# Gated MLP: weight tasks cut into parts, one part in each half block, and the later parts of next x loaded later

## The chip, the cores and the metric

The kernel runs on one core of a Trainium2 chip. The metric is the device time of one execution in microseconds (us). TensorE multiplies matrices and writes its results to PSUM; VectorE and ScalarE read PSUM; GpSimd does not. Each engine works through its own queue in order. All loads and stores of the stage looked at here are issued from SyncE's queue (SP).

## The reference

```python
# attention with exponential features, 8 batches, 8 heads, 576 tokens, 64 wide
num = einsum('bhsf,bhfd->bhsd', phi(q), einsum('bhsf,bhsd->bhfd', phi(k), v))
x = num / (einsum('bhsf,bhf->bhs', phi(q), phi(k).sum(2))[..., None] + 1e-06)   # -> (8, 576, 512)
# gated MLP
h = maximum(x @ w_in, 0)                       # 512 -> 1024
u, v = h[..., :512], h[..., 512:]
v_n = (v - mean(v)) / sqrt(var(v) + 1e-06)
v_s = einsum('ts,bsd->btd', w_spatial, v_n) + b_spatial[None, :, None]
x = (u * v_s) @ w_out                          # 512 -> 512
# mixer
u = x + (x.transpose(0, 2, 1) @ U @ V).transpose(0, 2, 1)     # rank 32 over the tokens
out = u + maximum(u @ w_ch1, 0) @ w_ch2                       # 512 -> 2048 -> 512
```

`w_in`, `w_out`, `U`, `V`, `w_ch1` and `w_ch2` come as 64-bit floats, the rest as 32-bit floats. The kernel turns the doubles into 32-bit floats on the chip. Products are taken in the rounded format `float32r`; each operand is split into a high and a low part, and three products (high high, high low, low high) are summed.

## The kernel before, in words

There are three stages: attention, the gated MLP (with the low-rank mixing), and the channel products with `w_ch1` and `w_ch2`. The change lies in the second, `gated_mlp`, which runs over the eight batches; its instructions are issued in the order in which the code writes them.

One batch of it has these steps on TensorE. `gate` computes **pu** (u = relu(x w_in)): four blocks f of 128 columns, each in two half blocks c of 288 tokens, 12 matmuls each. ScalarE evicts each half block (line 948). Then it computes **pz**, the spatial product: again four blocks in two halves, 14 matmuls each (lines 833 and 968). VectorE multiplies pz by u (line 972), ScalarE casts the product to its high part g, and GpSimd subtracts to get the low part; for the last block VectorE does that. Then comes **px**, the product with w_out in five token tiles, the low-rank sums **pr**, the values **pv** of the *next* batch between them (`ahead`), and `mixed`, which transposes (pt), adds the low-rank part (py) and stores u (tile `uo` to `ud`). The results pu, pz, px, pv and pt go to one pool of four PSUM banks: TensorE stops when the fourth result back has not been read.

In the second half of `gate` the next batch's x is loaded: four parts x32 of 128 rows, with two buffers; ScalarE casts each to its high part (line 872) and GpSimd subtracts the low part (line 869).

Beside this work the weights of the channel stage are prepared. `units` lists **tasks**, and seven of them are worked off in each batch: one behind each block of pu (`self.work()` in `gate`), one behind the first px tiles, and two in `mixed` (called m1 and m2 here). The kinds of task are:

- a *raw* task: 128 x 512 doubles, loaded to `raw` or `raw2` in turn by `fetch`, then turned into floats by `repack_doubles`: two ScalarE passes (`low`, line 110, and the size, line 112), then four VectorE passes (lines 113, 117, 120, 121). The tiles `low`, `bits` and the result `w32` have one buffer each. The result is stored to `w1d` or `w2r`, or kept in `w2`;
- `low_rank` and `v_stack`: the doubles of U and V, repacked, then copied to the stacked tiles ua, ub, vs;
- `pair(m)` and `left(m)`: sums of weight blocks on GpSimd (`left_sums`, tile z2) and their split into high and low parts (the tile of tag `w2s`, one buffer), stored to `w2d` and `w1x`. These are the operands of the fast block products of the channel stage.

A task's instructions all stand at one point. `flush` issues the stores that are due and then the loads of the next two raw tasks. It is called behind the first half block of each pu block and at two points behind pz, so SP's queue takes stores, raw loads and loads of x in that order.

After the last batch's pz, `first_chunk` loads u of the first chunk, `load_left` loads four weight tiles cw, and the channel stage's first products `hidden` (ph_x, ph_y, ph_z) start between the last batch's px and pt.

Of the kernel before, what the change touches and what calls it, by code (L numbers as in the profile page):

```python
# [9 lines left out]
F32 = mybir.dt.float32  # L10
# [90 lines left out]
def repack_doubles(nc, pool, dst, raw, name):  # L101


    n = dst.shape[1]
    pair = raw[:, : 2 * n].rearrange("p (c two) -> p c two", two=2)
    lo, hi = pair[:, :, 0], pair[:, :, 1]
    low, bits = (
        pool.tile([P, PIECE], I32, tag=t, name=f"{t}_{name}", bufs=1)[:, :n] for t in ("low", "bits")
    )
    nc.scalar.activation(low, lo.bitcast(U32), AF.Copy, scale=2.0**-29)  # L110
    size = lo.bitcast(F32)
    nc.scalar.activation(size, hi.bitcast(F32), AF.Square)
    nc.vector.tensor_scalar(
        out=bits, in0=hi, scalar1=3, scalar2=0x3FFFFFF8,
        op0=ALU.logical_shift_left, op1=ALU.bitwise_and,
    )
    nc.vector.scalar_tensor_tensor(
        out=bits, in0=hi, scalar=-0x40000000, in1=bits, op0=ALU.bitwise_and, op1=ALU.bitwise_or
    )
    nc.vector.tensor_tensor(out=bits, in0=bits, in1=low, op=ALU.add)  # L120
    nc.vector.scalar_tensor_tensor(
        out=dst, in0=size, scalar=TINY * TINY, in1=bits.bitcast(F32), op0=ALU.is_ge, op1=ALU.mult
    )


class Mixer:
# [175 lines left out]
    def fetch(self, parts, name):  # L302


        nc, raw = self.nc, None
        if any(src.dtype != F32 for _, src in parts):
            tag, pool = (("raw", self.sp), ("raw2", self.mq))[self.fetched % 2]
            self.fetched += 1
            raw = pool.tile([P, 2 * PIECE], I32, tag=tag, name=f"{tag}_{name}", bufs=1)
            for view, src in parts:  # L310
                nc.sync.dma_start(view(raw, 2), src.bitcast(I32))

        def into(dst):
            if raw is not None:
                return repack_doubles(nc, self.sp, dst, raw, name)
            for view, src in parts:
                nc.sync.dma_start(view(dst, 1), src)
        return into

    def units(self):  # L320


        nc, R, NF, HS, tail = self.nc, self.R, self.NF, self.HS, self.tail
        units = []

        def low_rank():
            c0, c1 = NF * R, (NF + 1) * R
# [1307 lines left out]
```

## Time and profile before

| | before |
|---|---|
| median of 3 runs | 1616.64 us (1614.0 to 1617.75) |
| the profiled execution | 1615.92 us |
| its span | 1614.1 us |
| TensorE busy | 1560.1 us, 97% of the span, 11592 matmuls |
| VectorE busy | 1112.1 us, 69% |
| ScalarE busy | 874.9 us, 54% |
| GpSimd busy | 797.2 us, 49% |
| DMA | 336.87 MB, mean 209 GB/s |

The span is the time between the first and the last instruction that the profiler saw, and the execution's own time is 1.8 us longer. "Busy" is the sum of instruction times of an engine. Ends of matmuls are modelled, so a busy TensorE need not be at its peak; a gap in its row is a real wait.

### The profile page before, as it was taken

What the parts mean: (1) busy time and instruction counts of PE and PEld (TensorE: products, weight loads), DVE (VectorE), ACT (ScalarE), POOL (GpSimd) and SP (SyncE); (2) the same over time, 40 slices, a digit from 0 to 9 for tenths busy, and PEclk for the clock granted to TensorE, in tenths of its full rate; (3) what the DMA queues carried; (4) which work ended last, traced back from release to release, by engine and by line L of the source; (5) the groups of instructions that cost most, each with busy time, mean ns of one, the idle gap of its engine ahead of it and who ended that gap; (6) DMA issues with size and microseconds to landing.
All of it is one profiled execution on the core that took longest, in us unless ns stands there. A gap on an engine that the chain in (4) does not pass through costs nothing.

```text
span 1614.1 us, 30569 instructions
## 1 busy us (share of the span) xinstructions
PE 1560.1 (97%) x11592; PEld 1469.5 (91%) x11592; DVE 1112.1 (69%) x1628; ACT 874.9 (54%) x1656; POOL 797.2 (49%) x610
## 2 busy tenths in 40 slices
PE   7999999998999999989999999999999999999998
PEld 7998888987888888878889999999999999999998
DVE  5888866875577677665675767777776666666656
ACT  4878768874444444434444555555554555554542
POOL 2677776775334343443523544455643533344433
PEclk9999999999999999999999999999999999999999
DMA  4677666753243343442526788989999877777786
GB/s 129 175 207 210 190 199 181 201 165 111 89 149 109 115 138 123 138 162 83 187 94 250 258 286 283 307 286 315 309 312 388 264 248 232 242 240 247 247 249 231
DMA packets 172278, 336.87 MB, mean 209 GB/s; under 512 B 25826, under 2 KB 96610, under 8 KB 169060
## 3 DMA queue, kind: packets, MB, share of 16 engines
q1 hardware_dynamic: 171988, 334.86, 65.0%
q8 instruction: 91, 1.49, 0.4%
q14 instruction: 55, 0.45, 0.1%
q10 hardware_dynamic: 144, 0.07, 0.0%
HBM read 251.73 MB, written 73.55 MB: 202 GB/s over the span
## 4 chain that ended last, share of the span: by engine, by line
PE 72%; DVE 9%; DMA 8%; ACT 4%; issue 3%; POOL 2%; SPq 1%; DVEq 0%; ACTq 0%; POOLq 0%
PE pc L833 19%; PE ph_x L833 11%; PE ph_z L833 6%; PE px L833 5%; PE pv L833 4%; PE pz L833 4%; PE pn L666 4%; PE pkv L638 3%; PE ph_y L833 3%; DMA den<-nd 2%; PE pu L833 2%; PE pk L565 2%; PE pt L597 1%; PE pq L565 1%; DMA raw_c<-in_w_ch 1%
## 5 line engine op out<-in xcount | busy, mean ns | idle before, releaser
L833 PE MATMUL pc<-hc,w 128*128 128x288 f32 x2688 | 423.2, 295 | 4.7 <-ACT hc L171 1.9
L833 PEld LDWEIGHTS pc<-hc,w 128*128 128x128 f32 x2688 | 379.0, 188 | 5.9 <-ACT us L171 2.1
L619 POOL TENSOR_TENSOR qp<-e,qp 128x576 fp32r<-128x576 f32 x128 | 183.5, 1455 | 118.7 <-ACT e L616 93.2
L833 PE MATMUL ph_x<-us,cw 128*128 128x288 f32 x1536 | 241.9, 295 | 0.1
L833 PEld LDWEIGHTS ph_x<-us,cw 128*128 128x128 f32 x1536 | 216.1, 188 | 1.0 <-ACT u L1272 0.5
L174 DVE TENSOR_TENSOR hc<-h,hc 128x576 fp32r<-128x576 f32 x192 | 191.8, 1002 | 34.1 <-ACT hc L171 34.0
L666 PE MATMUL pn<-qp,kv 128*65 128x288 f32 x768 | 207.1, 330 | 6.0 <-ACT nd L677 2.6
L1205 POOL TENSOR_TENSOR h<-h,h 128x576 f32<-128x576 f32 x64 | 108.0, 1690 | 132.2 <-DVE r L1441 126.2
L1205 POOL TENSOR_TENSOR t<-u,t 128x576 f32<-128x576 f32 x32 | 57.6, 1801 | 197.9 <-DVE c L1277 182.0
L638 PE MATMUL pkv<-v,kp 128*128 128x65 f32 x1024 | 154.6, 254 | 0.0
L638 PEld LDWEIGHTS pkv<-v,kp 128*128 128x128 f32 x1024 | 153.2, 193 | 0.0
L1272 ACT COPY u<-ph_x 128x288 f32<-128x288 f32 x128 | 51.1, 399 | 182.3 <-PE ph_x L833 182.3
L833 PE MATMUL ph_z<-us,cw 128*128 128x288 f32 x768 | 123.2, 296 | 10.0 <-DVE c L1277 10.0
L171 ACT CAST hc<-h 128x576 fp32r<-128x576 f32 x192 | 128.4, 672 | 6.6 <-PE pc L833 3.6
L1287 ACT ACTIVATE h<-c 128x288 f32<-128x288 f32 x192 | 85.2, 444 | 83.9 <-DVE c L1277 83.9
L833 PE MATMUL pz<-wt,vn 128*128 128x288 f32 x768 | 115.7, 300 | 11.6 <-DVE u L972 7.4
L833 PEld LDWEIGHTS pz<-wt,vn 128*128 128x128 f32 x768 | 107.7, 192 | 13.8 <-DVE u L972 8.4
L833 PEld LDWEIGHTS ph_z<-us,cw 128*128 128x128 f32 x768 | 108.4, 188 | 11.9 <-DVE c L1277 11.8
L904 POOL TENSOR_TENSOR rstd<-rstd,mhalf 128x1 f32<-128x1 f32 (+1 forms) x40 | 30.1, 753 | 168.6 <-DVE rstd L903 168.6
L666 PEld LDWEIGHTS pn<-qp,kv 128*65 128x65 f32 x768 | 99.2, 139 | 12.0 <-ACT nd L677 5.1
L833 PE MATMUL pu<-xs,wi 128*128 128x288 f32 x768 | 104.9, 298 | 4.9 <-ACT u L948 4.9
L833 PEld LDWEIGHTS pu<-xs,wi 128*128 128x128 f32 x768 | 104.3, 191 | 5.9 <-ACT u L948 5.1
(166 smaller groups left out, 3085.6 us busy)
## 6 DMA issues: line engine op xcount, KB each, us to landing
w<-w2d SPq DMA_DIRECT2D x224, 512.0 KB, 4.8
u<-ud SPq DMA_DIRECT2D x16, 1152.0 KB, 8.2
raw_c<-in_w_ch SPq DMA_DIRECT2D x32, 512.0 KB, 4.0
cw<-w1x SPq DMA_DIRECT2D x8, 1792.0 KB, 13.8
v<-in_v SPq DMA_DIRECT2D x32, 325.0 KB, 4.2
k<-in_kT SPq DMA_DIRECT2D x32, 320.0 KB, 3.5
q<-in_qT SPq DMA_DIRECT2D x32, 320.0 KB, 3.7
x<-nd SPq DMA_DIRECT2D x64, 144.0 KB, 3.3
```

The source lines that it names most:

```text
L171: self.put(nc.scalar.copy(hi, src))
L174: return self.put((nc.gpsimd if elo == "pool" else nc.vector).tensor_tensor(out=lo, in0=src, in1=hi, op=ALU.subtract))
L565: self.pin(nc.tensor.matmul(pa[:, j * NF + t, :], x[d, t * P : (t + 1) * P], ws[d, :], start=True, stop=True,))
L597: self.pin(nc.tensor.transpose(pt[:, at, :], s[:, u, :], self.ident))
L619: self.pin(nc.gpsimd.tensor_tensor(out=lo[:, c], in0=e[:, c], in1=hi[:, c], op=ALU.subtract))
L638: self.pin(nc.tensor.matmul(pkv[:, i, j, :], kp[:, j * NF + t, :], vb[:, u * D1 : (u + 1) * D1], start=False, stop=(j == 1 and t == NF - 1),))
L666: self.pin(nc.tensor.matmul(pn, kv[k][:, i, g // 2, :], qp[q][:, i, g * HS : (g + 1) * HS], start=(m == 0), stop=(m == len(terms) - 1),))
L833: self.put(self.nc.tensor.matmul(out, x, y, start=(start and i == 0), stop=(stop and i == len(terms) - 1), skip_group_check=chained,))
L904: nc.gpsimd.tensor_tensor(out=rstd[:n], in0=rstd[:n], in1=self.mhalf[:n, :1], op=ALU.pow)
L1205: x = self.put(self.nc.gpsimd.tensor_tensor(out=out, in0=p, in1=q, op=ALU.subtract))
L1272: self.put(nc.scalar.copy(out, src))
L1287: self.put(nc.scalar.activation(self.h[n, t // 2, x][:, t % 2], src, AF.Relu))
```

## The change

Each task is cut into parts, and each part gets a fixed place. A batch has the places 0 to 7 (the half blocks of pu), 8 to 15 (those of pz), "x" and "blocks" behind the first px tiles, and m1 and m2 in `mixed`. `work(b, place)` issues what the plan holds for that place.

- `repack_doubles` becomes the class `Repack` with `words` (the two ScalarE passes), `bits` (the first two VectorE passes) and `into` (the last two).
- `units` fills the plan: raw tasks mostly at the places (3, 4, 5), (6, 7, 8), (9, 10, 11), (12, 13, 14). Splits are cut into a high and a low part. U's copies stand at places 6 and 7 of batch 0, V's at 8 and 9. `left` and `pair` of a group are spread over three batches.
- `flush` is called behind every half block, and `work` after it.
- `normalize` is called behind the second half of each pu block, as before, and the small `pad` task moves from ahead of batch 0 to its place 3.
- The loads of parts 2 and 3 of next x stand behind the second half of pz blocks 1 and 2; they stood behind blocks 0 and 1.

```diff
-def repack_doubles(nc, pool, dst, raw, name):
...
+class Repack:
...
+    def words(self):
+        nc = self.nc
+        self.low, self.size = self.tile("low"), self.lo.bitcast(F32)
+        nc.scalar.activation(self.low, self.lo.bitcast(U32), AF.Copy, scale=2.0**-29)
+        nc.scalar.activation(self.size, self.hi.bitcast(F32), AF.Square)
+
+    def bits(self):
...
+        nc.vector.tensor_scalar(
+            out=bits, in0=hi, scalar1=3, scalar2=0x3FFFFFF8,
...
+        nc.vector.scalar_tensor_tensor(
+            out=bits, in0=hi, scalar=-0x40000000, in1=bits, op0=ALU.bitwise_and, op1=ALU.bitwise_or
+        )
+
+    def into(self, dst):
+        nc = self.nc
+        nc.vector.tensor_tensor(out=self.b, in0=self.b, in1=self.low, op=ALU.add)
+        nc.vector.scalar_tensor_tensor(
...
     def units(self):
...
+        def raw(load, b, places, store):
+            u = {}
+            def begin():
+                u["s"] = load()
+            self.raws.append([begin, False])
+            entry = self.raws[-1]
+            def end():
+                store(u["s"][2])
+                self.raws.remove(entry)
+            for place, f in zip(places, (lambda: u["s"][0](), lambda: u["s"][1](), end)):
+                at(b, place, f)
...
+        def halves(src):
+            d, n = self.mq.tile([P, 2, 4, HALF], F32R, tag="w2s", name=f"w2s_{self.made}", bufs=1), 0
...
+            def high():
+                for k, x in spans:
+                    nc.scalar.copy(d[:, 0, k], x)
+            def low():
+                for k, x in spans:
+                    nc.vector.tensor_tensor(out=d[:, 1, k], in0=x, in1=d[:, 0, k], op=ALU.subtract)
+            return d, n, high, low
...
         def pair(m, b, places):
...
+            at(b, 15, sums)
+            dst = lambda i, x: self.w2d[0][:, x, m, i, :]
+            part(lambda: [w[0][:, :, :HALF], w[0][:, 1, HALF:]], dst, 0, b, (15, "x"))
+            part(lambda: [z[0]], dst, 3, b, ("m1", "m1"))
...
         def left(m, b):
...
+            at(b, "blocks", load)
+            at(b, "m2", sums)
+            dst = lambda i, x: self.w1x[0][:, m, i, x]
+            part(lambda: [w[0][:, :3]], dst, 0, b, ("m2", "m2"))
+            part(lambda: [z[0]], dst, 3, b + 1, (2, 3))
...
+        usual = ((3, 4, 5), (6, 7, 8), (9, 10, 11), (12, 13, 14))
         half = self.DC // 2
+        raw(lambda: self.fetch(parts, "uv", c1 + HS), 0, (2, 4, 5), low_rank)
+        at(0, 3, self.pad)
+        at(0, 6, lambda: u_copies(0))
+        at(0, 7, lambda: u_copies(1))
+        at(0, 8, lambda: v_stack(0))
+        at(0, 9, lambda: v_stack(1))
+        first, others = columns(0) + columns(half), columns(PIECE) + columns(half + PIECE)
+        for x, places in zip(first, ((9, 10, 11), (12, 13, 14), ("m1",) * 3, ("m2",) * 3)):
+            piece(*x, 0, places)
+        for x, places in zip(first[4:], usual):
+            piece(*x, 1, places)
         for m in range(GROUP):
...
+            left(m, m + 1)
+            pair(m, m + 2, usual[:2])
+            for x, places in zip(others[2 * m : 2 * m + 2], usual[2:]):
+                piece(*x, m + 2, places)
+        for i in range(2):
+            for t in range(GROUP):
+                piece(*rows(GROUP + t + i * self.NM), 6 + i, usual[t])

     def flush(self):
...
+        for u in self.raws[:2]:
+            if not u[1]:
+                u[1] = True
+                u[0]()
+
+    def work(self, b, place):
+        for f in self.plan.pop((b, place), ()):
+            f()
...
                 nc.scalar.activation(u[:, c, :], pu[:, :HS], AF.Relu)
-                if c == 0:
-                    self.flush()
-            self.normalize()
+                self.flush()
+                if c:
+                    self.normalize()
+                self.work(b, 2 * f + c)
             us.append(u)
-            self.work()
...
-            if loads[f]:
-                loads[f]()()
-                if f + 2 < KD:
-                    loads.append(load(f + 2))
-            else:
-                loads.append(None)
+                self.flush()
+                if c and 1 <= f < KD - 1:
+                    loads.append(load(f + 1))
+                if c and loads[f]:
+                    loads[f]()()
+                self.work(b, 8 + 2 * f + c)
...
-            self.work()
+            self.work(b, "x")
             for t in range(NST):
...
                 if t == 1:
                     self.flush()
+                    self.work(b, "blocks")
...
             self.mixed(b, ts, t1, range(KD // 2))
-            self.work()
+            self.work(b, "m1")
```

Three places in the program show how the order moves. The first is ScalarE in pu of batch 1, before the change: line 948 evicts pu, lines 110 and 112 are the first passes of a raw task.

```order
L948 ACTIVATE u_0_5419<-pu_0_1_5437 128x288
L110 ACTIVATE low_c_1_1024_5456<-raw_c_1_1024_5346 128x512
L112 ACTIVATE raw_c_1_1024_5346<-raw_c_1_1024_5346 128x512
L948 ACTIVATE u_1_5464<-pu_1_0_5465 128x288
L948 ACTIVATE u_1_5464<-pu_1_1_5482 128x288
L110 ACTIVATE low_c_2_1024_5497<-raw_c_2_1024_5435 128x512
L112 ACTIVATE raw_c_2_1024_5435<-raw_c_2_1024_5435 128x512
L948 ACTIVATE u_2_5505<-pu_2_0_5506 128x288
```

The same stretch of ScalarE after the change (the lines are now 988, 116 and 117):

```order
L988 ACTIVATE u_0_5407<-pu_0_1_5425 128x288
L988 ACTIVATE u_1_5443<-pu_1_0_5444 128x288
L988 ACTIVATE u_1_5443<-pu_1_1_5458 128x288
L116 ACTIVATE low_c_0_1024_5472<-raw_c_0_1024_5334 128x512
L117 ACTIVATE raw_c_0_1024_5334<-raw_c_0_1024_5334 128x512
L988 ACTIVATE u_2_5475<-pu_2_0_5476 128x288
L988 ACTIVATE u_2_5475<-pu_2_1_5493 128x288
L988 ACTIVATE u_3_5510<-pu_3_0_5511 128x288
L116 ACTIVATE low_c_1_1024_5528<-raw_c_1_1024_5423 128x512
```

Two tasks instead of four begin in this pu, three evictions apart.

The second place is VectorE where pz of batch 1 begins. Before, four whole tasks stand ahead of the first product out of pz (line 972); these are the last rows of the fourth:

```order
L121 SCALAR_TENSOR_TENSOR w_c_3_1024_5537<-raw_c_3_1024_5480,bits_c_3_1024_5539 128x512
L113 TENSOR_SCALAR bits_c_0_0_5580<-raw_c_0_0_5521 128x512
L117 SCALAR_TENSOR_TENSOR bits_c_0_0_5580<-raw_c_0_0_5521,bits_c_0_0_5580 128x512
L120 ISA bits_c_0_0_5580<-bits_c_0_0_5580,low_c_0_0_5579 128x1024
L121 SCALAR_TENSOR_TENSOR w_0_5578<-raw_c_0_0_5521,bits_c_0_0_5580 128x512
L972 TENSOR_TENSOR u_0_5419<-pz_0_0_5593,u_0_5419 128x288
L972 TENSOR_TENSOR u_0_5419<-pz_0_1_5611,u_0_5419 128x288
L972 TENSOR_TENSOR u_1_5464<-pz_1_0_5633,u_1_5464 128x288
```

After, with line 1012 for the product and 122, 126, 132, 133 for the passes:

```order
L122 TENSOR_SCALAR bits_c_1_1024_5545<-raw_c_1_1024_5423 128x512
L126 SCALAR_TENSOR_TENSOR bits_c_1_1024_5545<-raw_c_1_1024_5423,bits_c_1_1024_5545 128x512
L1012 TENSOR_TENSOR u_0_5407<-pz_0_0_5554,u_0_5407 128x288
L132 ISA bits_c_1_1024_5545<-bits_c_1_1024_5545,low_c_1_1024_5528 128x1024
L133 SCALAR_TENSOR_TENSOR w_c_1_1024_5572<-raw_c_1_1024_5423,bits_c_1_1024_5545 128x512
L1012 TENSOR_TENSOR u_0_5407<-pz_0_1_5575,u_0_5407 128x288
L1012 TENSOR_TENSOR u_1_5443<-pz_1_0_5601,u_1_5443 128x288
L122 TENSOR_SCALAR bits_c_2_1024_5619<-raw_c_2_1024_5526 128x512
L126 SCALAR_TENSOR_TENSOR bits_c_2_1024_5619<-raw_c_2_1024_5526,bits_c_2_1024_5619 128x512
L1012 TENSOR_TENSOR u_1_5443<-pz_1_1_5622,u_1_5443 128x288
```

At most two passes stand between two products out of pz.

The third place is SP's queue around the end of batch 7: the last weight stores (to w2r), the load of the first chunk (u from ud) and the first cw. Before:

```order
L1051 DMA ud_71<-uo_3_2_9375 128x320
L481 DMA w1x_89<-w1s_1_9379 128x1024 x2
L481 DMA w2r<-w_c_15_9441 128x512
L1201 DMA u_0_9698<-ud_65 128x2304
L1142 DMA cw_9700<-w1x_89 128x3584
```

After:

```order
L1091 DMA ud_71<-uo_3_2_9346 128x320
L529 DMA w2r<-w_c_12_9471 128x512
L330 DMA raw_c_14_9490<-in_w_ch 128x1024
L529 DMA w2r<-w_c_13_9531 128x512
L330 DMA raw_c_15_9553<-in_w_ch 128x1024
L529 DMA w2r<-w_c_14_9597 128x512
L529 DMA w2r<-w_c_15_9661 128x512
L1241 DMA u_0_9698<-ud_65 128x2304
L1182 DMA cw_9700<-w1x_89 128x3584
```

Four stores of batch 7's own tasks, the last one issued behind place 14, now stand ahead of the load of u; before, one task was left for that batch.

## Rows read from the trace of the kernel before

**Rows 1.** TensorE's waits, 380 to 920 us: us in total, times, longest.

```profile
PE pz L833 <- DVE u L972: 7.4, 4, 5.1
PE pu L833 <- ACT u L948: 4.9, 1, 4.9
PE pz L833 <- ACT u L948: 4.2, 4, 1.5
...
PE px L833 <- POOL g L174: 1.9, 1, 1.9
```

**Rows 2.** Busy time by window: length, PE, PEld, DVE, ACT, POOL, clock, DMA.

```profile
386.48:452.92 66.44, 61.53 (x358) 54.82 (x357) 43.54 (x88) 30.69 (x69) 24.19 (x23) 0.97 0.26 84
452.92:517.42 64.50, 60.52 (x359) 53.35 (x357) 46.79 (x88) 27.53 (x57) 25.37 (x26) 1.00 0.36 122
517.42:578.20 60.78, 60.12 (x358) 53.24 (x357) 42.19 (x79) 26.95 (x55) 23.52 (x24) 1.00 0.37 118
578.20:639.52 61.32, 60.37 (x359) 53.37 (x358) 43.35 (x83) 27.21 (x56) 25.73 (x26) 1.00 0.43 136
639.52:700.73 61.21, 60.26 (x359) 53.32 (x357) 43.62 (x79) 26.54 (x55) 22.89 (x24) 1.00 0.41 128
700.73:768.89 68.16, 63.07 (x359) 56.13 (x357) 41.48 (x79) 26.51 (x54) 28.70 (x30) 0.95 0.42 144
768.89:832.45 63.56, 61.65 (x359) 54.26 (x357) 40.45 (x75) 26.68 (x54) 28.04 (x28) 0.97 0.40 131
832.45:860.02 27.57, 27.57 (x209) 27.57 (x208) 15.04 (x27) 8.06 (x18) 9.35 (x11) 1.00 0.30 113
485.25:517.42 32.17, 32.17 (x152) 25.70 (x150) 23.53 (x47) 14.40 (x30) 13.68 (x14) 1.00 0.25 85
```

**Rows 3.** The same view, the stretch behind batch 5's longest wait.

```profile
726.10:732.50 6.40, 6.36 (x27) 6.36 (x28) 1.54 (x4) 3.04 (x7) 5.87 (x7) 0.51 0.18 48
```

**Rows 4.** Timeline of ScalarE and VectorE, six moments: start, us, instruction [idle before, releaser].

```profile
399.36 0.32 ACT L352 CAST ua<-w_uv 128x160 fp32r<-128x160 f32 x1 [7.52 <-DVE w_uv L121]
...
462.52 1.51 DVE L113 TENSOR_SCALAR bits_c<-raw_c 128x512 int32<-128x512 int32 x1
...
465.62 0.67 ACT L110 ACTIVATE low_c<-raw_c 128x512 int32<-128x512 uint32 x1 [5.73 <-DVE bits_c L120]
...
699.06 0.84 ACT L171 CAST w1s<-w 128x768 fp32r<-128x768 f32 x1
...
723.90 0.83 ACT L171 CAST w1s<-w 128x768 fp32r<-128x768 f32 x1 [9.57 <-DMA raw_c<-in_w_ch]
...
794.53 0.68 ACT L872 CAST xs<-x 128x576 fp32r<-128x576 f32 x1 [4.82 <-DMA x<-xd]
```

**Rows 5.** Passes on raw tiles, 380 to 872 us: ns min/median/max.

```profile
L113 DVE TENSOR_SCALAR bits_c<-raw_c x32: 414/427/1508, 403.9 to 840.5; 128x512 int32<-128x512 int32 x32
L117 DVE SCALAR_TENSOR_TENSOR bits_c<-raw_c,bits_c x32: 691/693/1821, 404.4 to 842.1; 128x512 int32<-128x512 int32 x32
...
L121 DVE SCALAR_TENSOR_TENSOR w_c<-raw_c,bits_c x24: 691/693/1051, 406.2 to 843.7; 128x512 f32<-128x512 f32 x24
```

**Rows 6.** Groups by line and shape, VectorE, 380 to 870 us: busy us, mean ns.

```profile
L972 DVE TENSOR_TENSOR u<-pz,u 128x288 f32<-128x288 f32 x64 | 27.4, 452 | 45.1 <-PE pz L968 45.1
```

**Rows 7.** Timeline of GpSimd and VectorE behind pz of batch 1.

```profile
487.83 1.47 POOL L869 TENSOR_TENSOR xs<-x,xs 128x576 fp32r<-128x576 f32 x1 [0.49 <-ACT xs L872]
488.02 1.82 DVE L117 SCALAR_TENSOR_TENSOR bits_c<-raw_c,bits_c 128x512 int32<-128x512 int32 x1
```

**Rows 8.** DMA issues, 380 to 870 us: count, KB each, median us to landing.

```profile
w1x<-w1s SPq DMA_DIRECT2D x8, 512.0 KB, 5.2
```

**Rows 9.** End of batch 7: DMA issue of u (845 us), and timeline of SP, ScalarE.

```profile
u<-ud SPq DMA_DIRECT2D x1, 1152.0 KB, 5.1
...
860.26 1.82 SPq L1142 DMA_DIRECT2D cw<-w1x  x4
...
862.04 1.24 ACT L171 CAST us<-u 128x576 fp32r<-128x576 f32 x2
```

More of the change, by code (lines that the diff above doesn't have):

```diff
@@ new lines, in units, with at @@
+        self.raws, self.stores, self.waiting, self.plan = [], [], [], {}
+        def at(b, place, f):
+            self.plan.setdefault((b, place), []).append(f)
+        def raw(load, b, places, store):
[9 more added lines that the diff above has]
+                at(b, place, f)
@@ new lines, in units, with piece, store @@
+        whole = lambda t, s: t[:, : s * PIECE]
+        def piece(dst, src, name, b, places):
+            def store(into):
+                w = self.stage(name, PIECE)
+                into(w)
+                self.stores.append((dst, w))
+            raw(lambda: self.fetch([(whole, src)], name, PIECE), b, places, store)
+        parts = [(
+            lambda t, s: t[:, : s * c0].rearrange("p (k r) -> p k r", k=NF),
+            self.U[: NF * P, :].rearrange("(k p) r -> p k r", p=P),
+        )]
@@ new lines, in units, with part, first, second @@
+        self.made = 0
+        def part(src, dst, x0, b, places):
+            h = {}
+            def first():
+                h["d"], h["n"], high, h["low"] = halves(src())
+                high()
+            def second():
+                h["low"]()
+                for i in range(2):
+                    self.stores.append((dst(i, slice(x0, x0 + h["n"])), h["d"][:, i, : h["n"]].bitcast(F32)))
+            at(b, places[0], first)
+            at(b, places[1], second)
+        def pair(m, b, places):
@@ L386, in pair, with store @@
             w, z = [], []
-            def load(i):
+            for i in range(2):
                 r = slice((m + i * self.NM) * P, (m + i * self.NM + 1) * P)
-                into = self.fetch([(whole, self.w_ch2[r, :])], f"c2_{m}_{i}")
-                def step():
+                def store(into, i=i):
                     if i == 0:
@@ L446, in left, with sums @@
-            return [("blocks", load, True), (None, lambda: part(1), False)]
-        def rows(m):
-            return [
-                ("raw", piece(self.w2r[:, kk, :], self.w_ch2[kk * P : (kk + 1) * P, :], f"c2_{kk}"), False)
-                for kk in (m, m + self.NM)
-            ]
+            def sums():
+                z.append(self.mq.tile([P, 4, HALF], F32, tag="z2", name=f"z1_{m}", bufs=1))
+                self.left_sums([w[0][:, x] for x in range(4)], z[0])
+            at(b, "blocks", load)
@@ L1070, in gated_mlp @@
                 self.flush()
-                assert not self.todo
+                assert not self.plan and not self.raws
                 right.close()
```

233 lines of the change are left out of this document (81 added, 152 removed).

## The prediction

> **What bounds the kernel now.** I read the page first: TensorE is busy 97% of the span, so only time in which it waits or runs at a low clock can be won. The change lies in the gated MLP, about 386 to 875 us, so I next listed what TensorE waited for there, then cut that stretch into batches, then looked at the engines that were waited for.
>
> The waits of TensorE inside the stage that the change could touch are 7.4 + 4.9 + 4.2 + 1.9 = 18.4 us, all at evictions: pz waits until VectorE has multiplied an older pz out of its bank (line 972), pu and pz wait until ScalarE has evicted a pu (line 948), px for a low part on GpSimd [rows 1]. The windows run from the first pu matmul of one batch to that of the next [rows 2]. The last batch runs its pu and pz in 27.57 us with TensorE busy all the time, and the rest of a period takes 32.17 us in batch 1, again without a gap. A period without waits is thus 59.74 us. The seven periods are 66.44, 64.50, 60.78, 61.32, 61.21, 68.16 and 63.56 us, so they hold 6.70 + 4.76 + 1.04 + 1.58 + 1.47 + 8.42 + 3.82 = 27.8 us too much. That is more than the 18.4 us of waits, because the clock falls too: behind the longest wait, 5.1 us in batch 5, the granted clock is 0.51 for 6.40 us, the 1.2 GHz level instead of 2.4 [rows 3].
>
> Why an eviction is late is seen on the engine in front of it [rows 4]. ScalarE takes its queue in order. In batch 0 it stands 7.52 us before the copies of the low-rank weights, with finished pu blocks behind it. In batch 1 it stands 5.73 us before the first step of a weight task, which needs a buffer that VectorE still reads. In batch 5 it stands 9.57 us before a cast. The releaser named there is a raw load; by the code the cast writes the one buffer w2s, whose former content was still being stored, so I trust the place and not the name. In batch 6 it stands 4.82 us for a load of next x. In every case a whole weight task was put between two pu blocks, its first step waited, and evictions stood behind it.
>
> **The change part by part.** Call the 16 half blocks of a batch places 0 to 15: 0 to 7 are pu (12 matmuls each), 8 to 15 pz (14 each). 208 matmuls in 27.57 us make 0.1326 us each, so 1.59 us a place in pu and 1.86 in pz. T0 is the first pu of a batch.
>
> *No work is added.* The plan issues the same ScalarE, VectorE and GpSimd steps and the same DMAs; only their order differs. So the sum consists of waits that go and waits that come.
>
> *Waits that go.* A task's words (two ScalarE passes), bits (two VectorE passes) and the rest (two more) now stand one place apart. Nothing that waits in line for its data has a long chain in front: the buffer `low` is free again when the third part of the last task is done, one place before the next words. In batch 1 the fast times of the four VectorE passes are 0.43 + 0.69 + 0.69 + 0.69 us (for the third I take the time of the second) [rows 5], 2.50 us a task, and one product out of pz is 0.45 us [rows 6]. In batch 1 VectorE comes to its first pass behind the last token tile's normalisation at 462.52 us, T0 + 9.6 [rows 4]; with the two tasks before place 8 it comes to T0 + 14, where the first pz ends at T0 + 14.6. In pz it then has 8 x 0.45 for products, 7.5 - 1.1 for three tasks of which one has begun, and 2 x 0.45 (the same shape) for low parts of the last gated block, 10.9 of 14.84 us. It fits, so VectorE is late by no more than single places, and TensorE has four banks, that is three places or 5.6 us, before lateness reaches it. I count all 27.8 us as removed, and then what comes.
>
> *Batch 0.* u_copies still waits for the repacked low-rank weights, at 399.4 us as now, but it stands behind pu block 6 instead of blocks 2 to 7; only block 7 waits, about 1 us, within the banks. 0.5 us is left for the clock and small gaps.
>
> *Collisions in pz, batches 1 to 6.* A VectorE pass beside GpSimd's low parts can be much longer: a 0.69 us pass took 1.82 us when GpSimd began its x part 0.19 us before it [rows 7]. Three tasks a batch that lay mostly in pu now lie partly beside GpSimd's ten passes in pz. With some 0.4 us on each of ten passes VectorE needs 14.9 us instead of 10.9, as long as pz itself; what lateness comes of it the banks hide. I take 0.3 us a batch, 1.8 us; bounds 0 and the rival below.
>
> *The buffer w2s in batches 2 to 4.* It has one copy. In these batches the second half of a pair is split at m1, the first half of the next left weights at m2 and their second half at places 2 and 3, each waiting until the stores of the one before have landed. A pair of those stores takes 5.2 us at the larger size [rows 8]. In batch 5 ScalarE came to the cast that stood at m2 at 699.06 us, 1.7 us before T0 [rows 4]. VectorE's low part at m1 lies before that in the order, some 2 to 4 us before T0 (an estimate), so the stores land at T0 + 1.2 to 3.2, ScalarE stands 3 to 5 us and the evictions behind it come by T0 + 4. TensorE needs the bank of the last pv at T0 + 4.8. Hidden, narrowly; I take 0.4 us a batch, 1.2 us; bounds 0 and 4 a batch.
>
> *Next x.* Parts 2 and 3 are loaded two places before they are used, and no longer stand with part 0 and 1 in SP's queue. A load landed on time in the good batches, and a late one holds up only ScalarE's casts g and the low parts of the last block, which px needs only after its first 27 matmuls. The cost is 0; it takes away batch 6's wait, where the loads came late.
>
> *SP at the end of batch 7.* Now one weight task ends at place 14 of the last batch. Its store stands in SP's queue ahead of the load of the first chunk u and of the four cw loads. u used to be issued at T0 + 13, right after pu, and landed in 5.1 us; cw at 860.26 us, when pz ended [rows 9]. The last pz but one ends 1.86 us before pz does; a product, its cast and low part (0.45 each, by the product's row) and two passes of 0.69 follow, so VectorE ends that task about 1 us after pz, u goes out at pz + 1.4 and lands at pz + 6.5, and cw starts 1.6 us later behind 1152 KB of u. ScalarE's cast us<-u at 862.04 us, pz + 2, now waits until pz + 6.5 with the eviction of px behind it, GpSimd's sums begin as late, and I estimate that VectorE's chain of low parts up to the fifth hidden product ends 0.5 to 2 us later than TensorE wants it. The cw loads come some 4 us later; how much they have in hand no row shows, so 0 to 4. I take 1.3 us in all; bounds 0 and 6.
>
> Sum: -27.8 + 0.5 + 1.8 + 1.2 + 1.3 = -23.0 us. The profiled execution of 1615.92 us (span 1614.1 and 1.8 around it) becomes 1592.9. It lies 0.72 below the median of the runs, so against the median of 1616.64 the forecast is 1593.6 us.
>
> **The rivals.**
>
> *Forecast (0.76):* the waits go and small ones remain, 1588 to 1600 us.
>
> *The waits only move (0.15).* w2s lands late in batches 2 to 4 (two waits, 2 us each, 12 us) or the end of batch 7 costs its 6 us instead of 1.3. For it speaks the 9.57 us at just such a cast [rows 4]; against it that by the order raw loads were issued around those stores, which by the new plan are in before. 1593.6 + 12 = 1606 us; with a cheap m2 and a dear end 1598.
>
> *VectorE and GpSimd hold each other up in pz (0.05).* Mechanism: every pass of a task and both low parts fall on a GpSimd pass and lose the 1.13 us of the slow row, 12 passes, 13.6 us a batch. VectorE then needs 24.5 us for pz's 14.84; after the 5.6 us of banks TensorE waits 4.1 us a batch, and the px that needs the last low part about 1 us more. It decides from the point where a pass loses over a third of a us on average (3.9 over 12 passes) and VectorE's need passes pz. Seven batches make 36 us: 1616.6 - 27.8 + 36 + 1.3 = 1626 us. Against it: line 117 has a median of 0.693 with a maximum of 1.821 [rows 5], so most passes are untouched, though few of them lay in pz. The Trainium skill states the rule in "SBUF — State Buffer", section "Who interferes with whom": one pair of ports serves VectorE's second operand or fast mode and all of GpSimd, and whoever comes second is blocked to the end of the other's instruction. The pair of rows fits it, 1.82 us against 0.69 [rows 7]. By that rule alone GpSimd's later passes would be blocked as well, and the sum would be this rival's.
>
> *No change (0.04).* The plan's waits cost what it saves, through m1 and m2, where TensorE has no idle time now and where ScalarE would stand 6 us and more in every batch: 1613 to 1620 us.
>
> **How the numbers follow.** Runs of this kernel differ by under 0.2%, 3.2 us; within that no change can be told. Faster takes the forecast and the moved waits, with little of the rest: 0.90. Same 0.04, slower 0.06. The lower end of the range is all 27.8 us won, 1588.8, less a little for the run: 1588. The upper end takes in most of the second case: 1604. Outside lie some 0.05 below and 0.13 above.
>
> **What would show it.** Right: TensorE's waits in the stage fall from 18.4 us to under 4, no stretch at 1.2 GHz between 390 and 840 us, periods of 59.8 to 60.5 us, and a new wait of 0.5 to 2 us at the fifth hidden product after the last batch, with u<-ud issued after pz. Wrong: waits of pz on line 1012 in every batch would show the collisions; pv or pu waiting on ScalarE at the start of batches 3 to 5 would show w2s; a long wait of ph_x for cw would show SP's queue.

## The result, and the profile after

The changed kernel takes 1596.45 us (median of 4 runs, 1594.95 to 1598.42); the ratio to the kernel before is 0.9878, 95% interval 0.986 to 0.9896, that is 17 to 23 us less. The forecast was 1593.6 us. One run of the kernel before, at 1690.44 us, was slow and is left out. The profiled execution is the slowest of the four, 1598.42 us with a span of 1596.6.

TensorE's waits of the changed kernel in the window of [rows 1] (us in total, times, longest):

```profile
PE ph_z L873 <- DVE c L1317: 2.6, 1, 2.6
PE pr L1060 <- DVE xh L186: 0.7, 2, 0.5
PE pr L1062 <- DVE xl L187: 0.6, 3, 0.2
PE ph_x L873 <- DVE us L187: 0.3, 1, 0.3
```

Of the 18.4 us nothing is left: no pu, pz or px waits. The three small groups are new. The windows by batch, columns as in [rows 2]; the last line is batch 7's pu and pz:

```profile
388.57:448.32 59.75, 59.75 (x359) 53.27 (x357) 42.92 (x84) 30.06 (x68) 25.71 (x24) 1.00 0.25 81
...
627.54:687.31 59.77, 59.77 (x359) 53.27 (x358) 47.39 (x80) 27.96 (x56) 30.36 (x29) 1.00 0.46 155
687.31:747.44 60.13, 60.03 (x358) 53.31 (x357) 47.85 (x80) 28.04 (x56) 30.96 (x29) 1.00 0.41 139
...
807.21:834.78 27.57, 27.57 (x210) 27.57 (x208) 19.77 (x34) 11.49 (x24) 8.91 (x10) 1.00 0.26 89
```

Six of seven periods are 59.74 to 59.77 us, batch 5's is 60.13, and the granted clock is 1.00 throughout: the stretch at 0.51 of [rows 3] has no successor. From the first pu of batch 0 to the first px of batch 7 it was 860.02 - 386.48 = 473.54 us and is 834.78 - 388.57 = 446.21: 27.33 won. The span fell by only 17.5, so 9.8 came back: 2.09 ahead of the first pu and 7.74 behind the first px of batch 7 (754.08 us to the end before, 761.82 now). The timeline of SP, ScalarE and TensorE at that end answers to [rows 9]:

```profile
829.96 6.26 SPq L529 DMA_DIRECT2D w2r<-w_c  x2
836.33 0.37 SPq L1241 DMA_DIRECT2D u<-ud  x1
838.20 2.05 SPq L1182 DMA_DIRECT2D cw<-w1x  x4
...
842.11 1.25 ACT L184 CAST us<-u 128x576 fp32r<-128x576 f32 x2 [4.41 <-DMA u<-ud]
843.27 0.58 ACT L1046 COPY x<-px 128x512 f32<-128x512 f32 x1
...
849.68 0.49 PE L1060 MATMUL pr<-xh,ua 128*128 128x512 f32 x1 [0.50 <-DVE xh L186]
850.40 0.50 PE L1062 MATMUL pr<-xl,ub 128*128 128x512 f32 x1 [0.23 <-DVE xl L187]
...
852.06 1.64 PE L873 MATMUL ph_x<-us,cw 128*128 128x288 f32 x6
```

SP stands 6.26 us over two stores; the second needs the last pass of the task at place 14. So u leaves 1.55 us behind pz (it left 14.6 us ahead of the end of pz before), ScalarE stands 4.41 us for it with the eviction of px behind, and TensorE waits at pr in pieces of 0.2 to 0.5 us. The granted clock falls there too. The first two windows of the changed kernel below begin with the pr matmuls, the last one holds the wait of ph_z:

```profile
847.78:852.58 4.80, 3.49 (x9) 1.94 (x10) 4.59 (x10) 1.12 (x2) 0.41 (x1) 0.84 1.01 430
847.78:864.78 17.00, 15.37 (x85) 12.98 (x86) 14.33 (x25) 7.57 (x17) 2.97 (x2) 0.90 0.84 351
...
878.78:890.78 12.00, 9.36 (x59) 9.12 (x58) 9.24 (x12) 7.57 (x17) 5.79 (x4) 0.86 0.87 299
```

Six matmuls of ph_x take 1.64 us, where six take 0.95 to 0.96 at full clock: the granted clock was 0.50 from 852.06 to 853.50 us, the 1.2 GHz level. The pr matmuls that wait show something else, with the clock still at full speed. In the kernel before they follow each other by 0.23 us:

```profile
872.79 0.39 PE L1020 MATMUL pr<-xh,ua 128*128 128x512 f32 x1
873.02 0.39 PE L1022 MATMUL pr<-xl,ub 128*128 128x512 f32 x1
```

Now the ones at 849.68 and 850.40 us start 0.72 us apart. Only 0.23 of this is counted as a wait, the other 0.49 as the matmul at work. So a wait here costs more than the profile counts for it. Counted from the first px of batch 7, the first hidden product starts at 17.28 us (before: 14.13) and the first pt at 26.82 (22.22).

### The profile page after: what moved, and what is told of

Same layout as the page of the kernel before. It is cut to its first block, busy times and chain, and to the rows that moved or that the text cites. A ratio compares the mean times of both kernels' runs of the same rounds, so it can differ in the third digit from the quotient of the medians.

```text
span 1596.6 us, 30554 instructions
## 1 busy us (share of the span) xinstructions
PE 1556.6 (97%) x11592; PEld 1467.3 (92%) x11592; DVE 1133.2 (71%) x1628; ACT 875.8 (55%) x1656; POOL 812.0 (51%) x610
## 4 chain that ended last, share of the span: by engine, by line
PE 80%; DMA 8%; DVE 5%; ACT 3%; issue 2%; SPq 1%; POOL 0%; DVEq 0%; ACTq 0%; POOLq 0%
PE pc L873 18%; PE ph_x L873 11%; PE pu L873 6%; PE pz L873 6%; PE pv L873 6%; PE ph_z L873 6%; PE px L873 5%; PE pn L706 4%; PE pkv L678 4%; PE ph_y L873 3%; DMA w<-w2d 2%; PE pk L605 2%; PE pt L637 1%; PE pt L1082 1%; PE pz L1008 1%
## 5 line engine op out<-in xcount | busy, mean ns | idle before, releaser
L706 PEld LDWEIGHTS pn<-qp,kv 128*65 128x65 f32 x768 | 100.1, 141 | 14.1 <-DVE nd L715 6.0
L873 PE MATMUL pz<-wt,vn 128*128 128x288 f32 x768 | 112.0, 295 | 0.0
L1481 DVE TENSOR_TENSOR r<-pc,r 128x576 f32<-128x576 f32 x111 | 83.7, 754 | 30.2 <-PE pc L873 29.6
```

The costliest lines, as they stand in the source:

```text
L706: self.pin(nc.tensor.matmul(pn, kv[k][:, i, g // 2, :], qp[q][:, i, g * HS : (g + 1) * HS], start=(m == 0), stop=(m == len(terms) - 1),))
L873: self.put(self.nc.tensor.matmul(out, x, y, start=(start and i == 0), stop=(stop and i == len(terms) - 1), skip_group_check=chained,))
L1481: self.read = self.put(nc.vector.tensor_tensor(out=r, in0=pc, in1=r, op=ALU.add)).ins
```

## The experiments

The first four runs ask what costs the time behind batch 7. Theory A: the missing microseconds are the late load of u. Theory B: that part is longer by chance or by other transfers. From "the moved load alone" on, the question is what wins the 27 us. In the first four, differences are to the run `again`, the changed kernel measured beside them; in the others they go by the ratios to the kernel before, which was measured beside each group; 0.001 of ratio is 1.6 us. "The stage" is the time from the first pu of batch 0 to the first px of batch 7, in the profiled execution: 473.54 us before, 446.21 in the changed kernel, 446.75 and 445.98 in two more profiles that have its tasks and places (`again` and `x_as_before`).

**The changed kernel once more** (no edit).

> The changed kernel once more, as the measure for the others of this call. Theory A (the end of batch 7 costs): the profile shows again no wait of TensorE in pu, pz and px of the eight batches, periods of 59.7 to 60.2 us, and from the first px of batch 7 to the fourth group of hidden products (the first pt) 26.8 us where the kernel before needs 22.2; 1595 to 1598 us. Theory B (the part behind px is longer by chance or by the transfers of that moment): the first pt comes at 22 to 24 us behind the first px this time. For the head, the first pu of batch 0: at 386 to 389 us, since nothing ahead of it was changed; the 2.1 us by which it came later in the profile of after should come and go.

1595.03 us (6 runs), ratio 0.9879 (0.9856 to 0.9902). First pu at 386.91, so the 2.1 us ahead of it were not the change's. First px to first pt 26.44 us: again long, against B. To the end 759.84.

**u earlier.** The first two lines stand in `gate`, behind the last pu:

```diff
+        if b == self.B - 1:
+            self.u_first = self.first_chunk()
...
-                u = self.first_chunk()
+                u = self.u_first
```

> Only the load of the first chunk u is issued elsewhere: behind the last pu of batch 7, ahead of the stores and raw loads of its pz places, instead of behind the store of place 14. Theory A: u leaves when pu ends and lands before pz ends; ScalarE's cast us<-u no longer holds up the eviction of px; TensorE has no wait at the pr matmuls (1.4 us in after) nor at the fourth ph_x (0.3), no clock under 1.00 there, and the first pt stands 22.2 us behind the first px instead of 26.8. With the second low stretch, behind the wait of ph_z, gone too that is 4.6 + 1.3 us: about 1590.5 us (1589 to 1592.5), 6 below the changed kernel of the same call. Theory B: u was not what was waited for; within 1 us of the changed kernel, the first pt again at 26 to 27 us.

1590.69 us (5 runs), ratio 0.9846 (0.9822 to 0.987): 4.3 less than the changed kernel measured beside it. TensorE's waits in the same stretch, then SP and ScalarE:

```profile
PE ph_z L873 <- DVE c L1319: 2.7, 1, 2.7
PE ph_x L873 <- DVE us L187: 0.8, 1, 0.8
PE pv L885 <- ACT uo L1091: 0.3, 1, 0.3
```

```profile
818.12 0.32 SPq L1243 DMA_DIRECT2D u<-ud  x1
...
835.92 1.25 ACT L184 CAST us<-u 128x576 fp32r<-128x576 f32 x2 [0.27 <-DMA w2r<-w_c]
```

No wait at pr is left, the first hidden product is at 14.13 us as before the change, the first pt at 23.11. A holds. The gain lies below the 6 us expected: ph_x now waits 0.8 us, and the low clock behind ph_z, which the expectation counted as gone, came here too.

**u later.**

```diff
-                u = self.first_chunk()
-                for m in range(GROUP):
+                self.load_left(0)
+                u = self.first_chunk()
+                for m in range(1, GROUP):
```

> The dose in the other direction: one cw load of 1792 KB is put ahead of the load of u. At the 400 to 440 GB/s of that stretch it takes 4.1 to 4.5 us, so u lands that much later. Theory A: the chain from u over us, the eviction of px, xh and xl to pr has no hand left in it, so everything behind it is later by the same 4 us or a little more, the clock lower for longer: the first pt 30 to 33 us behind the first px, 1600 to 1604 us. Theory B: no change within 1 us, since the chain has slack or cw is what is waited for.

1601.4 us (6 runs, 1596.45 to 1606.71), ratio 0.9911 (0.9885 to 0.9938): 6.4 more. One wait of TensorE and one of ScalarE:

```profile
PE px L885 <- ACT x L1046: 3.7, 1, 3.7
```

```profile
842.75 1.25 ACT L184 CAST us<-u 128x576 fp32r<-128x576 f32 x2 [10.07 <-DMA u<-ud]
```

ScalarE stands 10.07 us instead of 4.41, the eviction of px comes so late that TensorE now stops in px itself, the first pt comes at 32.43. Both doses move the end the way A says.

**x loaded as before, in the changed kernel.**

```diff
-                if c and 1 <= f < KD - 1:
-                    loads.append(load(f + 1))
                 if c and loads[f]:
                     loads[f]()()
+                if c and f + 2 < KD:
+                    loads.append(load(f + 2))
```

> The changed kernel with the loads of parts 2 and 3 of next x put back behind pz blocks 0 and 1. Theory C (only the weight tasks mattered): SP's queue is flushed at every half block and never long, so x still lands in time or holds up nothing but ScalarE's casts; no wait of TensorE in the stage, within 1.5 us of the changed kernel. Theory D (the moved load is what removed batch 6's wait): the period of batch 6, and perhaps others, is again 1 to 4 us over 59.74, with TensorE waiting for VectorE or ScalarE in pz; 1598 to 1604 us.

1595.52 us (6 runs), ratio 0.9868 (0.9843 to 0.9894), periods 59.74 to 59.85 us: C. Within the plan the moved load is worth nothing.

**The moved load alone, in the kernel before.**

```diff
-            if loads[f]:
-                loads[f]()()
-                if f + 2 < KD:
-                    loads.append(load(f + 2))
-            else:
-                loads.append(None)
+            if 1 <= f < KD - 1:
+                loads.append(load(f + 1))
+            if loads[f]:
+                loads[f]()()
```

> The kernel before with only the loads of parts 2 and 3 of next x moved, as in the change. Theory D: batch 6's wait goes (ScalarE's 4.82 us for x, a period 3.8 us too long): periods else as before, 3 to 4 us below the kernel before. Theory C: the loads stand as late in SP's queue behind weight stores, the wait only moves: within 2 us of the kernel before, or some us slower because part 3 is used one block behind its load.

1616.91 us (12 runs), ratio 1.0004 (0.9988 to 1.0021). ScalarE in batch 6, by the timeline:

```profile
794.00 0.67 ACT L872 CAST xs<-x 128x576 fp32r<-128x576 f32 x1 [4.70 <-DMA x<-xd]
```

It stands as before (4.82, [rows 4]): the late load is part 0's, in SP's queue behind four block loads of `left`, a raw load and two split stores. Batch 6 is 1.9 us shorter in this profile, but the wait is still there: TensorE waits 1.6 us at px where it was 1.9, and the granted clock is 1.00 over the period where it was 0.97. D falls: no gain shows in the total.

**Tasks whole, in the changed kernel's places.**

```diff
-            for place, f in zip(places, (...)):
+            for place, f in zip(places if store is low_rank else places[:1] * 3, (...)):
```

> The changed kernel's places, but every raw task stands whole at the first of its three places (only U and V keep their three): tasks still begin three half blocks apart. Theory S (it is the spacing and the places that count): 3 places are 4.8 to 5.6 us and a task is 2.5 to 3.6 us of VectorE, so the next words wait for nothing; in pz a product stands behind four passes instead of two, 2.5 to 3.6 us, and the banks give 5.6; no wait of TensorE in pu, pz and px, periods of 59.7 to 60.5 us, within 2 us of the changed kernel (1595). Theory C (the cut in parts counts): evictions stand behind whole tasks again, TensorE waits 1 to 3 us a batch for u on VectorE in pz, with low clock behind it: 1600 to 1612 us.

1610.85 us (12 runs), ratio 0.9961 (0.9948 to 0.9975): 13 us of the gain lost. S falls and the size is C's, but the next run shows that the four passes are not the main cause. The stage takes 464.23 us, 18.0 more than in the changed kernel; the end of batch 7 gets shorter, because the last task now ends at place 12 (first hidden product at 14.23 us). Waits in the stage, of TensorE, ScalarE and VectorE, and SP, ScalarE and VectorE in pz of batch 1:

```profile
PE pz L873 <- DVE u L1012: 7.5, 5, 2.5
...
ACT xs L912 <- DMA x<-xd: 28.4, 13, 5.0
...
DVE bits_c L132 <- ACT low_c L116: 21.4, 8, 4.2
```

```profile
463.16 0.62 SPq L330 DMA_DIRECT2D raw_c<-in_w_ch  x1
465.75 0.32 SPq L529 DMA_DIRECT2D w1d<-w_c  x1
466.18 0.37 SPq L330 DMA_DIRECT2D raw_c<-in_w_ch  x1
466.64 0.89 SPq L905 DMA_DIRECT2D x<-xd  x2
...
471.91 0.67 ACT L912 CAST xs<-x 128x576 fp32r<-128x576 f32 x1 [4.99 <-DMA x<-xd]
472.49 0.66 ACT L116 ACTIVATE low_c<-raw_c 128x512 int32<-128x512 uint32 x1
...
473.18 1.45 DVE L132 CUSTOM_DVE_ANT_0 bits_c<-bits_c,low_c 128x1024 uint16<-128x1024 uint16 x1 [3.88 <-ACT low_c L116]
474.71 0.69 DVE L133 SCALAR_TENSOR_TENSOR w_c<-raw_c,bits_c 128x512 f32<-128x512 f32 x1
475.32 1.18 DVE L1012 TENSOR_TENSOR u<-pz,u 128x288 f32<-128x288 f32 x3
```

Read it from the bottom: three products out of pz stood behind a pass that waited for ScalarE's words, the words behind a cast that waited for x, and the load of x behind a store and a raw load. A task that ends two places earlier has its store and the next raw load put ahead of x, where the changed kernel has them behind it. That store could leave only when VectorE's last pass of the task was done (465.72 us), and SP takes its queue in order. So x left 3.0 us later than in the changed kernel, counted from the batch's first pu, and then took 5.3 us to land where it takes 3.9 there (medians of the loads in pz of batch 1).

**Whole tasks, x first.** The edit above, and parts 0 and 1 of next x are loaded at the first half of pu block 2 (`load_x` takes these tiles then; not shown):

```diff
+                if f == 2 and c == 0 and b + 1 < self.B:
+                    for kk in range(2):
+                        x32 = self.early[b + 1, kk] = self.wp.tile(...)
+                        nc.sync.dma_start(x32, self.xd[b + 1][:, kk, :])
                 self.flush()
```

> Whole raw tasks at the first of their places, as before, but parts 0 and 1 of next x are loaded earlier: issued at the first half of pu block 2, so that no raw load of pz stands in front of them. With whole tasks the load of x came behind two raw loads, ScalarE stood up to 5 us at the cast of x with the words of the next task behind it (28.4 us of such waits), and VectorE for those words (21.4 us). Theory X (that queueing on SP is the loss of whole tasks): ScalarE's waits for x fall under 8 us, VectorE's for the words under 8 us, TensorE's for pz under 2; periods 59.8 to 60.8 us, 1595 to 1600 us. Theory Q (four passes in one piece, or two casts ahead of them, are the loss): the waits of pz stay at 7 us or more, 1605 to 1611 us.

1597.61 us (6 runs), ratio 0.9883 (0.9858 to 0.9909). ScalarE and VectorE:

```profile
ACT xs L914 <- DMA x<-xd: 6.8, 7, 2.3
```

```profile
DVE bits_c L132 <- ACT low_c L116: 2.8, 4, 0.8
```

No wait of TensorE in pz is left. X: with the tasks still whole, all but 2.5 us of the stage's loss is back (448.69 us, against 464.23 with whole tasks and 446.21). In the total it is nearer to the changed kernel than that, because the first hidden product comes at 14.13 us here.

**Only VectorE's passes whole.**

```diff
-            for place, f in zip(places, (...)):
+            for place, f in zip(places if store is low_rank else (places[0], places[2], places[2]), (...)):
```

> The changed kernel with only VectorE's part of the cut undone: the words (ScalarE) stay at the first place of a task, all four passes of VectorE stand at the third. Theory L (in the run with whole tasks VectorE lost its time waiting for ScalarE's words, 21.4 us in all, with products out of pz queued behind): here the words lie two places ahead, so VectorE waits for nothing, and four passes (2.5 to 4 us beside GpSimd) stay under the 5.6 us of the banks: no wait of TensorE in pz, periods of 59.7 to 60.3 us, within 2 us of the changed kernel (1595). Theory Q (the four passes in one piece are what is too long): waits of pz for VectorE as with whole tasks, 7 us and more over the stage, 1600 to 1611 us.

1602.38 us (6 runs), ratio 0.991 (0.9883 to 0.9937): some 5 us lost, and neither theory has the place. There are no waits in pz. Batches 2 to 5 are 1.3 us longer each, all behind pz: the windows from px to the next pu, here and (second fence) in the changed kernel:

```profile
532.70:566.15 33.45, 33.01 (x152) 25.62 (x150) 25.89 (x48) 14.17 (x31) 14.40 (x15) 1.00 0.42 135
```

```profile
535.63:567.80 32.17, 32.17 (x152) 25.70 (x150) 23.84 (x46) 12.72 (x27) 12.51 (x13) 1.00 0.36 118
```

The banks hide the four passes in pz, but the task at place 14 now has all of them there, VectorE works 2 us more behind px and comes late to xh and xl, and pr waits (TensorE's only wait between 500 and 752 us):

```profile
PE pr L1062 <- DVE xl L187: 1.8, 8, 0.2
```

That is 0.44 us a batch, and it costs 1.28: TensorE is also busy 0.84 us longer for the same matmuls, at a granted clock of 1.00. At the end of batch 7 the first hidden product is at 19.32 us.

**Tasks two places apart, in parts and whole.**

```diff
-        usual = ((3, 4, 5), (6, 7, 8), (9, 10, 11), (12, 13, 14))
+        usual = ((1, 2, 3), (3, 4, 5), (5, 6, 7), (7, 8, 9))
```

> The changed kernel with tasks in three parts, but two half blocks apart instead of three: places (1,2,3), (3,4,5), (5,6,7), (7,8,9). A raw buffer comes free at the end of a task, so the load of the next but one leaves at place 4 and is used at place 5, 1.6 us later, where a raw load takes 3.6 us to land. Theory S: ScalarE stands 2 us or more before the words of the third and the fourth task of each batch, with evictions of pu behind it; of that TensorE sees 0 to 3 us a batch; 1597 to 1612 us, periods up to 63 us. Theory C: the cut suffices, since only two passes stand ahead of any eviction; 1595 us, periods as in the changed kernel.

> As the run with places two apart, but with every raw task whole at its first place (1, 3, 5, 7): the arrangement nearest to the kernel before, with the rest of the plan (U and V late, splits spread, stores at every half block) left as it is. Here a load leaves at place 2, 4 for use at 5, 7: 4.8 us, in time. VectorE's four passes are 2.5 us in each 3.2 us of pu, beside the normalisation of the last token tile. Theory S: as in batch 1 before, VectorE falls behind in pu and the first products come late: 1 to 4 us a batch, 1600 to 1615 us. Theory E (the four single events of before, in batches 0, 1, 5 and 6, made up the loss, and the rest of the plan removes all but batch 1's): 0 to 1 us a batch, 1595 to 1600 us.

In parts 1603.61 us (6 runs), ratio 0.9913 (0.9898 to 0.9929), periods 61.1 to 63.7 us in batches 1 to 5; whole 1616.83 us (12 runs), ratio 1.0001 (0.9986 to 1.0017). The stage takes 460.32 us in parts, 14.1 more than in the changed kernel, and 470.33 whole. The total in parts hides much of that: with no task behind place 9 the end of batch 7 is as before the change (first hidden product at 14.13 us, first pt at 22.21, in both). Waits of TensorE and ScalarE, in parts:

```profile
PE pz L873 <- ACT u L988: 11.4, 10, 1.9
...
ACT low_c L116 <- DVE bits_c L132: 31.3, 7, 5.7
...
ACT low_c L116 <- DMA raw_c<-in_w_ch: 28.1, 13, 3.8
```

S holds, C falls: parts do not help a ScalarE that stands before their first step. They do help VectorE. With whole tasks TensorE's waits in pz are

```profile
PE pz L873 <- ACT u L988: 10.4, 9, 1.6
PE pz L873 <- DVE u L1012: 8.3, 6, 1.6
```

and the second group is what the cut takes away, 10.0 us of the stage. Whole and crowded, nothing of the gain is left in the total, though U and V, the splits and the flushes are as in the change; E falls, and the loss is a little above S's range. One part of the gain stays in every variant: batch 0 takes 59.75 to 60.47 us in all of them, where it took 66.45, whether tasks are cut, whole or crowded. What they share there is that the copies of U and V stand late: ScalarE waits 1.3 us for those weights in the changed kernel, 1.1 with whole tasks and 0.9 with whole and crowded ones, where it was 7.52 [rows 4].

**The last tasks moved.**

```diff
+        slots = [(6, x) for x in usual] + [(6, ("m1",) * 3), (6, ("m2",) * 3), (7, usual[0]), (7, usual[1])]
+        for k, (b, places) in enumerate(slots):
+            i, t = divmod(k, GROUP)
+            piece(*rows(GROUP + t + i * self.NM), b, places)
```

> The changed kernel with the last two weight tasks of batch 7 taken out of its pz: the fifth and sixth of the eight w2r tasks stand whole at m1 and m2 of batch 6, the last two at the first six places of batch 7's pu, so the last store is out at place 9 and nothing but that stands ahead of u. Theory A: u leaves when pu ends, as with the load put forward; first hidden product 14.1 us behind px, first pt at 22.2; 1590 us (1588.5 to 1592.5). VectorE has no passes in that pz, so the 0.8 us that the fourth ph_x still waited with the load put forward goes too. The rival: whole tasks at m1 and m2 hold up evictions of pt and pv there and cost 1 to 5 us in batch 6: 1591 to 1597 us.

> Both mends together: the last tasks moved to m1 and m2 of batch 6, and the load of u issued behind the last pu. Theory A: they mend the same thing, so the gains don't add: 1588.5 to 1592.5 us, the part behind the first px of batch 7 at 754 to 756 us as in the kernel before, against 758.5 to 761.8 in the changed kernel. If they add, two different losses were in it: 1585 to 1587 us.

1591.1 us (6 runs), ratio 0.9848 (0.9824 to 0.9873), and with u put forward as well 1592.61 us (6 runs), ratio 0.9851 (0.9825 to 0.9878). First pt at 22.21 and 22.22 us. The rival falls: batch 6's period is 59.76 us in the one and 59.74 in the other profile, so the whole tasks at m1 and m2 cost nothing there. (Batch 5's is 60.76 and 59.74; it is the one that varies in the profiles of the changed kernel too, 60.13 and 60.58.) The gains don't add, so they mend one thing. All three mended versions beat both kernels by their medians; among the three no difference can be told.

## Why the prediction was right or wrong

*The waits that go: right.* Forecast 27.8 us. The periods are 0.46 us in all above 59.74 x 7, so with 27.3 won practically all went. The argument for it was half right. It blamed whole tasks between evictions. Measured in the stage, tasks in parts but two places apart lose 14.1 us, and whole tasks three places apart with x loaded first lose only 2.5: cutting alone is not it. Nor is it worth nothing: two places apart it wins 10.0 us, and with the four passes whole at the last of the three places 4.8 are lost behind px. What counts most is that a task's first step does not stand waiting, and with it the evictions behind: tasks three places apart, and x ahead of a task's store and the next raw load, or the task cut so that these come behind x. Of batch 0's 6.7 us at least 6.0 are won in every variant, where the copies of U and V stand late. What spreading the splits and the more frequent flushes are worth by themselves no run shows.

*Batch 0, collisions, w2s: forecast 0.5 + 1.8 + 1.2 = 3.5 us, measured 0.5.* All three mechanisms are there and stayed hidden. Passes on raw tiles as in [rows 5], and pz of batches 2 and 3 as windows:

```profile
L126 DVE SCALAR_TENSOR_TENSOR bits_c<-raw_c,bits_c x32: 691/693/1884, 410.1 to 832.1; 128x512 int32<-128x512 int32 x32
...
L133 DVE SCALAR_TENSOR_TENSOR w_c<-raw_c,bits_c x24: 691/694/1283, 412.2 to 835.2; 128x512 f32<-128x512 f32 x24
```

```profile
520.78:535.63 14.85, 14.85 (x114) 14.85 (x113) 11.71 (x18) 7.68 (x16) 9.73 (x9) 1.00 0.62 196
580.52:595.37 14.85, 14.85 (x114) 14.85 (x113) 13.07 (x20) 8.82 (x17) 9.23 (x9) 1.00 0.60 193
```

VectorE is busy 11.7 and 13.1 of pz's 14.85 us, where the step had 14.9. The rival in which each pass loses 1.13 us is out: the medians did not move. The means did, by groups of line and shape (busy us, mean ns):

```profile
L126 DVE SCALAR_TENSOR_TENSOR bits_c<-raw_c,bits_c 128x512 int32<-128x512 int32 x32 | 31.3, 978 | 1.1
...
L187 POOL TENSOR_TENSOR g<-u,g 128x288 fp32r<-128x288 f32 x48 | 45.7, 954 | 68.6 <-ACT g L184 68.6
```

Before they were 824 and 816 ns: on either engine instructions got longer on average, and TensorE has no wait in pz for it. The Trainium skill's rule ("SBUF — State Buffer", "Who interferes with whom") says that whoever comes second is blocked, on either engine, and these means agree; by that rule for every pass the sum was the rival's 1626 us, and the time is not. ScalarE's waits for w2s are at most 2.5 us, where 3 to 5 were estimated, and in batch 0 it stands 1.3 us for the weights, where about 1 was forecast.

*Next x: cost 0, right; "it takes away batch 6's wait", wrong.* In the kernel before the moved load changes neither that wait nor the time, in the changed kernel putting it back costs nothing. What changed is the queue ahead of part 0: four block loads, a raw load and two split stores before, one store and one raw load now. Part 0 left 18.1 us behind batch 6's first pu and now leaves at 11.2. That this is what took the wait away fits the rows; no run moved these transfers alone.

*SP at the end of batch 7: the mis-sized term.* Forecast 1.3 us, with bounds 0 and 6. The chain was right to the engine: u out at pz + 1.4 (measured 1.55), landed by pz + 6.5 (ScalarE goes on at 7.3), the cast in front of the eviction of px, cw in time. What failed is the estimate that VectorE's chain is only 0.5 to 2 us late, and at the fifth hidden product. It is late from the first pr on, 1.38 us in five waits, plus 0.32 at the fifth group of hidden products (ph_x). The first pt comes 4.60 us later (4.22 and 4.68 in two other profiles with this end), and for the other 2.9 us the step had no term. The clock is one part: at 0.90 over 17 us it takes 1.7 us at most (an estimate from that row). The rest, 1.2 us or more, is there at full clock as well: the pr matmuls that wait stand 0.72 us apart where only 0.23 of it is counted as a wait, and the run with only VectorE's passes whole shows 0.84 us a batch of this kind at a clock of 1.00. To the end of the program the three profiles show 7.7, 5.8 and 4.4 us more than before; the run with u earlier gives 4.3 back in the time. What lies behind the first pt is not of this term: see the last section.

The forecast of -23.0 so holds +3.5 of which 0.5 came, and 1.3 where 4 or more came: two errors of some 3 us that cancel, which is luck. The measured change is -20.2 us (17 to 23 by the interval); the 2 to 3 us between are not accounted for, and the time ahead of the first pu alone varies by more. The prediction's "under 0.2%, 3.2 us" for the spread of runs is a little low too: the three runs it had spread over 3.75 us, 0.23%.

## What to carry to other kernels

Before weighing how long a queued step is, ask what its first instruction waits for, and what stands behind it: the same whole tasks cost 2.5 or 18 us of the stage by which transfer left first on a shared queue. A task that ends earlier sends its store and the next load earlier, and can so delay somebody else's load; move a load and look at the others in its queue. Compare variants stage by stage: the one with crowded tasks lost 14 us in the stage and 5.5 in the total, because it mended the end by the way. At the end of a loop check which store now stands ahead of the next stage's first load, and price the small waits it makes above what the profile counts: the matmuls around them take longer, and the clock can fall.

## What the hardware showed that was not expected

- The first pu of batch 0 came at 383.67 to 392.93 us in the 12 profiles of the changed kernel and its variants, with the attention stage ahead of it untouched. So the total of one profile is good to some 5 us either way, while the period of a batch without waits agreed to 0.06 us.
- The same wait does not always cost the same. The first wait of ph_z for VectorE behind batch 7 was 2.6 to 2.7 us in each profile compared; in the 12 us that hold its end the granted clock was 1.00 in the kernel before, in `again` and with the last tasks moved, and 0.86 in the profiled execution of the changed kernel, with u earlier and with both mends. From the first pt to the first pc it took 24.6 us in the former and 25.3 to 25.9 in the latter.
- Most of a load's lateness came before it left. With whole tasks the loads of x in pz of batch 1 took 5.3 us to land and in the changed kernel 3.9, but the first of them had left 3.0 us later, behind a store that waited for VectorE.
